# First layer of a two-level fast matrix product: six of nine steps taken in pairs with 256 moving columns, and their x^T blocks built in place

## The chip, the cores and the metric

One core of one Trainium2 chip runs the whole kernel. The metric is device time in microseconds (us) of one execution; lower is better. Three executions of the kernel before took 1302.05, 1302.54 and 1305.91 us; their median is 1302.54 us. One further execution was profiled.

## The reference

Threshold attention over 8 batches of 8 heads (576 positions, head size 64) gives x with 4608 rows of 512. Then a feed-forward block with a squared ReLU follows; all is fp32:

```python
h = np.maximum(x @ w_in, 0.0)        # 4608x512 @ 512x2048: the first layer
return (h * h @ w_out)               # 4608x2048 @ 2048x512: the output layer
```

## The kernel before

**Three stages.** Attention comes first (0 to 506 us) and writes x transposed, xT, to DRAM. The first layer runs from 506 to 900 us, the output layer from 900 us to the end. The change is in the first layer.

**First layer.** The 4608 rows are cut into nine steps of 512 (NSTEP, STEP). Each step is a two-level fast product of the kind that needs 7 block products where the plain rule needs 8: the outer level has seven indices m in the order OUTER = 1, 2, 6, 7, 4, 5, 3 (L130), and within each there are seven inner indices k, so a step has 49 products. Below, "index i" means the i-th of OUTER (i = 0 to 6), and "place (i, at)" the point in the program after the at-th product (0 to 6) of index i. A pass over all seven indices is one call of hidden_layer (L828).

**One product** (L838) takes a 128x512 weight block W_IN[m, k] (four stationary 128x128 pieces) and an x^T block of 128 rows by 128 tokens (the moving operand), so four matmuls of 128 columns fill one PSUM bank of 512 columns. In the trace every fp32 matmul is two records, each a weight load and a matmul.

**Taking results out.** `inner` (L717) runs the seven products of an index in the order k = 1, 6, 7, 5, 2, 4, 3. The banks are named X, Y, Z, W, out of a ring of six. ScalarE copies X to p1 (L752). VectorE adds Y to p1, giving u2, and Z to u2, giving u3, and then takes each finished block out of PSUM with an add (all at L125). Products 5, 6 and 7 accumulate onto X, Z and W, so product 5 waits until p1 is copied, product 6 until u3 is made, and product 7 until the first finished block, (1, 1), has been read from W. GpSimd adds earlier partial results (L125): none at index 0 (m = 1), six at index 5 (m = 5), three at every other. The temporaries p1, u2, u3 and the three sums come from a ring of six.

**Squaring.** The 16 finished blocks of a step (four each at m = 2, 4, 5, 3) are put on a list and squared six products later or more (squares_due, L823): Relu and Square on ScalarE (L819, L820), then a store of 256 KB to gT in DRAM from SP's queue (L821).

**x^T.** Each step's x^T takes four 256 KB parts from DRAM (load_x, L761) into seven slots of 512 columns, one for each m, and a side area for the three made inner kinds. There are two such regions (X_AT, L101), used in turn, so step n+1 is built while step n is multiplied. prepare_x (L789) makes 12 sums a step; each goes through sum_v (L777): ScalarE copies one operand to a PSUM buffer c (L786, two buffers), and one place later VectorE adds (L122). They run at places (2, 0) to (5, 5), one half of a sum at each place. The first step's sums are made on GpSimd during attention.

**Beside it.** 44 "chains" (L1113) make sums of w_out blocks through DRAM: a load, four GpSimd subtractions of 128x128 six to nine places later (L122), and a store at place ten. They start at places 0, 6, 12, 18, 24, 30 of a step (CHAINS, L1067). In the last step the blocks of w_out replace W_IN in SBUF (reload, L1056).

**What sets the order.** The schedule is written by hand: each engine runs its instructions in program order, and a semaphore wait holds everything behind it on that engine. All loads and stores named above go through SP's queue, in program order too. `tick` (L877), after every product, calls `also` (L1148: chains and x^T sums) and then squares_due.

Of the kernel before, what the change touches and what calls it, by code (L numbers as in the profile page):

```python
# [48 lines left out]
def kernel(  # L49
# [25 lines left out]
    nc = tc.nc  # L75
    B, H, S, D = q.shape
    P = 128
# [7 lines left out]
    BANK = 512  # L85
    MAIN = FULL * P
    STEP = 512
    NSTEP = B * S // STEP
# [6 lines left out]
    gT = [[dram.tile([P, BANK], FP32, name=f"g{n}_{j}") for j in range(16)] for n in range(NSTEP)]  # L95
# [25 lines left out]
    def minus(e, out, x, y):  # L121
        e.tensor_tensor(out=out, in0=x, in1=y, op=ALU.subtract)  # L122
# [10 lines left out]
    AT_A, AT_B = ((1, 2), (7, 4)), ((1, 7), (2, 3))  # L133
# [4 lines left out]
    W_IN, W_OUT = {}, {}  # L138
# [619 lines left out]

    XPARTS = ((0, 0), (1, 0), (1, 1), (0, 1))

    def load_x(n, parts=XPARTS):  # L761
        at = X_AT[n % 2]
        xo = arena[:, ds(at, 7 * BANK)].rearrange("p (m c t) -> p m c t", m=7, c=2)
        for a, c in parts:
            to = xo[:, AT_B[a][c] - 1, :, :]
# [9 lines left out]
        prepared[n] = (xo, None)  # L775

    def sum_v(op, out, x, y):  # L777

        c = b_pool.tile([P, BANK], FP32, tag="b", name="c")
        n = 1
        for m in y.shape[1:]:
            n *= m
        c = c[:, 0:n].rearrange("p (a b) -> p a b", b=y.shape[2])
        nc.scalar.copy(c, y)  # L786
        return lambda: op(nc.vector, out, x, c)

    def prepare_x(n, add):  # L789
# [19 lines left out]
                    yield  # L809
        prepared[n] = of  # L810

    hid = Region(arena, 0, 26 * BANK)
    squares, clock = deque(), {"n": 0}
    def hidden_bank():
# [2 lines left out]
    def square(n, j, o):  # L817

        nc.scalar.activation(out=o, in_=o, func=AF.Relu)  # L819
        nc.scalar.activation(out=o, in_=o, func=AF.Square)  # L820
        nc.sync.dma_start(out=gT[n][j][:, :].rearrange("p (k t) -> p k t", k=4), in_=o)  # L821

    def squares_due(wait):  # L823

        if squares and squares[0][0] + wait <= clock["n"]:
            square(*squares.popleft()[1:])

    def hidden_layer(n, also):  # L828

        of = prepared.pop(n)  # L830
        tile4 = lambda tag, bufs: hid.tile([P, 4, NQ], FP32, tag=tag, bufs=bufs)
        bank = lambda: hidden_bank()[:, :].rearrange("p (k t) -> p k t", k=4)
        temp = lambda name: tile4("t", 6)
        U2, U3 = {}, {}

        for m in OUTER:

            def product(to, k, more):  # L838
                for j in range(4):
                    nc.tensor.matmul(  # L840
                        to[:, j, :], W_IN[m, k][:, ts(j, P)], of[k][:, m - 1, :], start=(not more and j == 0), stop=True,
                        skip_group_check=True,
                    )

            def add(to, c, other, more, t=None):

                if other is None:
                    plus(nc.vector, to, c, more)
                else:
                    plus(nc.gpsimd, to, t, more)  # L850

            def final(ab, c, other):
                if m == 1:
                    U2[ab] = tile4("u", 12)
                    if other is None:
                        nc.scalar.copy(U2[ab], c)
                    else:
                        plus(nc.vector, U2[ab], c, other)
                    return
                t = None  # L860
                if other is not None:
                    t = temp("t")
                    plus(nc.vector, t, c, other)
                if m == 6:
                    add(U2[ab], c, other, U2[ab], t)
                elif m == 7:
                    U3[ab] = tile4("u", 12)
                    add(U3[ab], c, other, U2[ab], t)
                else:
                    o = tile4("o", 8)  # L870
                    add(o, c, other, U3[ab] if m in (4, 5) else U2[ab], t)
                    if m == 5:
                        add(U2[ab], c, other, U2[ab], t)
                    row, col = {2: (0, 0), 4: (1, 0), 5: (1, 1), 3: (0, 1)}[m]
                    squares.append((clock["n"], n, 4 * (2 * row + ab[0]) + 2 * col + ab[1], o))

            def tick(at):  # L877
                clock["n"] += 1
                also(m, at)
                squares_due(6)  # L880

            inner(product, copy, temp, bank, final, tick)


# [132 lines left out]
    with tc.manual_schedule():  # L1017
# [46 lines left out]
        halves_ = [(m, k, h) for m, k in blocks_out[EARLY:] for h in range(2)]  # L1064
        chains = [((0, RAW.index(k)), c) for k in RAW for c in range(4)]
        chains += [((1, made_at(m)), c) for c in range(4) for m in OUTER]
        CHAINS = [49 * n + 6 * c for n in range(NSTEP - 1) for c in range(n == 0, 6)][0 : len(chains)]  # L1067
        QUARTER = BANK // 4
        two = lambda t: t.rearrange("p (k o) -> p k o", k=2)
        raw_out = {}  # L1070
# [58 lines left out]
                if s_ == 10:  # L1129
                    nc.sync.dma_start(out=on(4), in_=t)  # L1130

        for n in range(NSTEP):
            last = n == NSTEP - 1
            if not last:
                load_x(n + 1)
                xsums = prepare_x(n + 1, sum_v)
            else:
                load_g(0, [(m, k) for m in (7, 4, 1, 2) for k in K_ORDER])
                rest = lambda: None
                first, second_one = outer_sums(0, 5, (1, 2))  # L1140
                work = {
                    2: outer_sums(0, 5, (7,)) + outer_sums(0, 6, (7,)),
                    3: outer_sums(0, 3, (7,)) + outer_sums(0, 7, (7,)),
                    4: inner_sums(0, 1),
                    6: [rest, rest, first, rest, second_one, rest, rest],
                }

            def also(m, at):  # L1148
                i = OUTER.index(m)
                convert_out(n, 7 * i + at)  # L1150
                chain_out(n, 7 * i + at)
                if not last:
                    if 2 <= i <= 5 and at < 6:
                        next(xsums)
# [5 lines left out]
            hidden_layer(n, also)  # L1160
            if not last:
                next(xsums, None)
        for n in range(NSTEP):
            more = n + 1 < NSTEP

            def work_of(i):

                work = [] if i == 6 else inner_sums(n, OUTER[i + 1])
                if (n, i) == (0, 0):
                    work += outer_sums(0, 6, (1, 2)) + outer_sums(0, 5, (4,)) + outer_sums(0, 6, (4,))  # L1170
                if (n, i) == (0, 1):
                    work += outer_sums(0, 7, (1, 2, 4)) + outer_sums(0, 3, (1, 2, 4))
                if more and i == 4:
                    work += outer_sums(n + 1, 5) + outer_sums(n + 1, 7, (7, 1))
                if more and i == 5:
                    work += outer_sums(n + 1, 6) + outer_sums(n + 1, 7, (2, 4))
                if more and i == 6:
                    work += outer_sums(n + 1, 3) + inner_sums(n + 1, 1)
                return work

            def also(m, at):
                i = OUTER.index(m)
                if n == 0 and 7 * i + at < 10:
                    reload(39 + 7 * i + at)
                if more and (i, at) == (2 if n == 0 else 0, 0):
                    load_g(n + 1, [(m_, k) for m_ in KINDS[0:2] for k in K_ORDER])
                if at == 0:
                    work[0] = work_of(i)
                spread(work[0], at)
                if at > 4:  # L1190
                    squares_due(0)
# [47 lines left out]
```

## Time and profile before

| | |
|---|---|
| median of three runs | 1302.54 us |
| profiled execution | 1302.09 us, of which the span from the first to the last instruction is 1300.3 us |
| first layer (L840), 1764 matmuls, 3528 records | 506.0 to 900.0 us, 394.0 us |
| one step, one index, one product | 43.78 us, 6.25 us, 0.894 us |
| granted TensorE clock | 0.998 over the span |

A line of a page names the line of the kernel, the engine (PE is TensorE's matmul, PEld its weight load, DVE VectorE, ACT ScalarE, POOL GpSimd, SP the queue of transfers), the output and inputs, and the count; then busy time, the mean duration of one, and the idle time ahead of it with what ended that. A PE duration is not a cost: matmuls overlap, so the distance from one start to the next is the measure.

### The profile page before, as it was taken

To read this page: it belongs to the slowest core of one execution; us is meant where nothing else is said; L and a number is where in the kernel's file an instruction comes from. 1 tells how busy PE (TensorE), PEld (TensorE's weight loads), DVE (VectorE), ACT (ScalarE), POOL (GpSimd) and SP (SyncE) were. 2 spreads that over 40 slices of the span, in tenths; PEclk is the share of its full clock that TensorE was granted. 3 is DMA by queue.
4 is the path that set the end of the run, shared out by engine and by line. 5 is a ranking of instruction groups with operands and counts; after the bars stand their busy time and mean duration, and the time that the engine had idled before them with its cause. 6 is when DMAs were issued, how large, how long until landed. Compare 5 with 4: busy or idle time off the path is not lost.

```text
span 1300.3 us, 47830 instructions
## 1 busy us (share of the span) xinstructions
PE 1280.6 (98%) x19463; PEld 1157.1 (89%) x19463; DVE 1009.3 (78%) x2431; ACT 846.5 (65%) x1498; POOL 916.7 (71%) x1023
## 2 busy tenths in 40 slices
PE   8999999999999999999999999999999999999998
PEld 5777777777777778999999999999999999999998
DVE  6999999999999995877787778777646654665463
ACT  6999999989998984757675766575523432343240
POOL 2787787755555321977897879768777767777775
PEclk9999999999999999999999999999999999999999
DMA  6656666544333312556655765579645224522411
GB/s 154 168 144 156 161 186 183 142 106 110 82 87 78 89 33 67 164 182 222 200 166 186 227 195 164 163 280 390 218 158 163 85 84 159 162 77 91 159 34 34
DMA packets 247035, 192.12 MB, mean 148 GB/s; under 512 B 97184, under 2 KB 195488, under 8 KB 246816
## 3 DMA queue, kind: packets, MB, share of 16 engines
q1 hardware_dynamic: 245504, 188.66, 48.5%
q8 instruction: 153, 2.51, 0.8%
q14 instruction: 66, 0.54, 0.1%
q10 hardware_dynamic: 1312, 0.41, 0.1%
HBM read 116.65 MB, written 72.35 MB: 145 GB/s over the span
## 4 chain that ended last, share of the span: by engine, by line
PE 91%; ACT 4%; DVE 3%; DMA 2%; issue 1%; POOL 0%; ACTq 0%; POOLq 0%; SPq 0%; DVEq 0%
PE ph L840 30%; PE po L975 29%; PE sc L532 11%; PE sc L434 10%; PE pt L380 6%; DVE arena L452 2%; PE sc L515 2%; PE sc L398 2%; ACT arena L523 1%; ACT arena L462 1%; DMA wall<-w 1%; PE sc L380 1%; DMA g<-arena 0%; ACT arena L403 0%; PE idle L1027 0%
## 5 line engine op out<-in xcount | busy, mean ns | idle before, releaser
L125 POOL TENSOR_TENSOR arena<-arena 128x512 f32<-128x512 f32 (+1 forms) x314 | 377.7, 1222 | 133.3 <-DVE arena L125 115.2
L975 PE MATMUL po<-wall,arena 128*128 128x128 f32 x3528 | 394.9, 275 | 1.4 <-ACT arena L752 1.4
L975 PEld LDWEIGHTS po<-wall,arena 128*128 128x128 f32 x3528 | 394.3, 192 | 2.0 <-ACT arena L752 1.8
L840 PE MATMUL ph<-arena,wall 128*128 128x128 f32 x3528 | 394.2, 275 | 0.7 <-DVE arena L659 0.7
L840 PEld LDWEIGHTS ph<-arena,wall 128*128 128x128 f32 x3528 | 394.0, 192 | 0.8 <-issue 0.8
L125 DVE TENSOR_TENSOR arena<-ph,arena 128x512 f32<-128x512 f32 x378 | 256.4, 689 | 86.2 <-PE ph L840 66.3
L122 POOL TENSOR_TENSOR arena<-arena 128x128 f32<-128x128 f32 (+2 forms) x314 | 254.7, 812 | 50.2 <-DMA arena<-w 33.8
L125 DVE TENSOR_TENSOR arena<-po,arena 128x128 f32<-128x128 f32 x378 | 108.3, 290 | 167.9 <-PE po L975 163.7
L467 DVE SCALAR_TENSOR_TENSOR arena<-arena 128x576 f32<-128x576 f32 x288 | 235.4, 853 | 0.7 <-ACT arena L462 0.7
L462 ACT ACTIVATE arena<-arena 128x576 f32<-128x576 f32 x288 | 208.6, 773 | 7.5 <-DVE arena L452 4.2
L452 DVE TENSOR_SCALAR_CACHE_REDUCE arena<-sc 128x576 f32<-128x576 f32 x288 | 205.2, 748 | 10.4 <-ACT arena L523 4.2
L786 ACT COPY c<-arena 128x512 f32<-128x512 f32 (+1 forms) x303 | 173.5, 579 | 50.1 <-DVE arena L122 41.3
L532 PEld LDWEIGHTS sc<-arena 64*64 64x64 f32 x5760 | 158.8, 133 | 35.6 <-DVE arena L452 19.4
L532 PE MATMUL sc<-arena 64*64 64x128 f32 (+1 forms) x5760 | 179.3, 262 | 2.7 <-DVE arena L452 1.5
L434 PE MATMUL sc<-arena 64*64 64x64 f32 (+1 forms) x2304 | 176.5, 414 | 3.4 <-ACT arena L403 2.3
L122 DVE TENSOR_TENSOR arena<-arena,c 128x512 f32<-128x512 f32 (+1 forms) x267 | 174.9, 663 | 5.9 <-ACT c L786 4.0
L523 ACT COPY arena<-pt 128x1024 f32<-128x1024 f32 x144 | 146.4, 1017 | 27.5 <-PE pt L380 26.3
L752 ACT COPY arena<-po 128x128 f32<-128x128 f32 x63 | 16.7, 264 | 186.5 <-PE po L975 183.7
L380 PEld LDWEIGHTS pt<-ident,arena 64*128 64x128 f32 x2304 | 83.4, 139 | 40.4 <-ACT arena L523 29.3
L752 ACT COPY arena<-ph 128x512 f32<-128x512 f32 x63 | 36.6, 582 | 124.3 <-PE ph L840 123.8
L434 PEld LDWEIGHTS sc<-arena 64*64 64x64 f32 x2304 | 74.2, 134 | 41.4 <-issue 14.4
L380 PE MATMUL pt<-ident,arena 64*128 64x64 f32 x2304 | 102.3, 229 | 3.6 <-ACT arena L523 2.2
(51 smaller groups left out, 918.7 us busy)
## 6 DMA issues: line engine op xcount, KB each, us to landing
g<-arena SPq DMA_DIRECT2D x144, 256.0 KB, 2.4
arena<-g SPq DMA_DIRECT2D x144, 256.0 KB, 4.6
w<-arena SPq DMA_DIRECT2D x60, 256.0 KB, 2.4
wall<-w SPq DMA_DIRECT2D x49, 256.0 KB, 5.2
arena<-w SPq DMA_DIRECT2D x44, 256.0 KB, 3.4
arena<-in_v_dram SPq DMA_DIRECT2D x32, 288.0 KB, 4.0
out_dram<-arena SPq DMA_DIRECT2D x70, 128.0 KB, 2.3
arena<-in_q_dram SPq DMA_DIRECT2D x64, 128.0 KB, 3.9
```

What stands on the lines that cost most here:

```text
L122: e.tensor_tensor(out=out, in0=x, in1=y, op=ALU.subtract)
L125: e.tensor_tensor(out=out, in0=x, in1=y, op=ALU.add)
L380: made = nc.tensor.transpose(pt[:, r, ts(slot, HALF)], of[rows, :], ident[rows, rows])
L434: made = nc.tensor.matmul(sc[at, ds(to, count)], lhs, kT[rows, ds(at_k, count)], start=True, stop=True)
L452: made = nc.vector.tensor_scalar(out=s[:, j, :], in0=sc[:, ds(at, S)], scalar1=1.0, scalar2=None, op0=ALU.mult, op1=ALU.min, accum_out=nmx ...
L462: nc.scalar.activation(out=w[:, :, j, :], in_=of(j), func=AF.Exp, bias=nmx[:, j : j + 1], scale=-1.0)
L467: nc.vector.scalar_tensor_tensor(out=w[:, :, j, :], in0=of(j), scalar=thr[:, j : j + 1], in1=w[:, :, j, :], op0=ALU.is_le, op1=ALU.mult, a ...
L523: touch("weights", nc.scalar.copy(joined(to), whole(pt, 0, count)), at, 2 * BANK, m)
L532: made = nc.tensor.matmul(sc[ds(u * D, D), ds(5 * j * BANK + row, count)], loaded_v[i][rows, (c - (u != j)) % CH, :], wT[m][rows, ds(weigh ...
L786: nc.scalar.copy(c, y)
L840: nc.tensor.matmul(to[:, j, :], W_IN[m, k][:, ts(j, P)], of[k][:, m - 1, :], start=(not more and j == 0), stop=True, skip_group_check=True,)
L975: nc.tensor.matmul(to, g[:, j, :], w[:, j, :], start=(not more and j == 0), stop=(j == 3), skip_group_check=True)
```

## The change

The nine steps become nine passes: step 0 alone; steps 1 and 2, 3 and 4, 5 and 6 in pairs, two passes to a pair; steps 7 and 8 alone. In a pair's pass a product loads only two of the four weight pieces (half h of the output columns) and moves 256 columns, 128 of each step, in two runs that lie one region (X_SIZE) apart. So a pass still has 49 products, each filling one bank, but with two matmuls in place of four.

Since a pair holds both regions, the next pair's x^T cannot be built in a free one. It is built in place: before_x runs in the pass ahead of a pair (passes 0, 2, 4, 6) and within_x in the pair's first pass (1, 3, 5, and 7 for steps 7 and 8). Each loads a part when its slot's index m has been multiplied, and sums over both steps at once. Sums still go through sum_v, one half of one at each place (advance_x). The sums for m = 1 and 2 run at places (5, 6) to (6, 6) of the pass ahead; those for m = 6 and 7 at (0, 6) to (1, 6), for m = 4 and 5 at (2, 4) to (3, 4), and for m = 3 at (4, 0) to (5, 0). One outer difference a step goes to GpSimd, at place (0, 1).

The squarings of m = 3, the last index, are due four products later (LATER). A pair's block holds two steps, so its store is two of 128 KB, in runs of 128 columns. Chains start at places 6, 12, 18, 24, 36 and 45 of a pass (the last as -4 of the next). The attention stage and the output layer's instructions stay.

```diff
+    def part_x(steps, k, m, count=None):
+        of = slice((steps[0] + 1) % 2, (steps[0] + 1) % 2 + len(steps))
+        ms = slice(m - 1, m - 1 + count) if count else m - 1
+        if k in (1, 7, 2, 3):
+            return places_x[:, of, ms, k in (2, 3), k in (7, 3), :]
+        return sums_x[:, of, (5, 6, 4).index(k), ms, :]
...
+    def outer_x(steps, op, o, x, y):
+        return [lambda n=n: sum_v(op, slot_x(n, o), slot_x(n, x), slot_x(n, y)) for n in steps]
+
+    def inner_x(steps, m, count=2):
+        of = lambda k: part_x(steps, k, m, count)
+        return [
+            lambda op=op, o=o, x=x, y=y: sum_v(op, of(o), of(x), of(y))
+            for op, o, x, y in ((minus, 5, 7, 1), (minus, 7, 3, 7), (plus, 6, 7, 1), (minus, 4, 2, 6))
+        ]
...
+    BEFORE_X = {(1, 0): (1, 1), (2, 0): (3, 2), (2, 1): (7, None), (3, 6): (2, 2), (6, 0): (3, 5)}
+
+    def before_x(steps, i, at):
+        if (i, at) in BEFORE_X:
+            ask_x(steps, *BEFORE_X[i, at])
...
+        if i == 4 and at < len(steps):
+            nc.scalar.copy(slot_x(steps[at], 7), slot_x(steps[at], 6))
+        work = {
+            (3, 0): lambda: turned_()[0:1], (3, 3): lambda: turned_()[1:],
+            (4, 2): lambda: added()[0:1], (4, 5): lambda: added()[1:],
+            (5, 1): lambda: fourth()[0:1], (5, 4): lambda: fourth()[1:],
+            (5, 6): lambda: inner_x(steps, 1),
+        }
+        return work.get((i, at), list)()
+
+    def within_x(steps, i, at):
+        if (i, at) == (0, 0):
+            ask_x(steps, 3, 3)
+        if (i, at) == (0,1):
+            for n in steps:
+                minus(nc.gpsimd, slot_x(n, 5), slot_x(n, 5), slot_x(n, 6))
+        work = {
+            (0,6): lambda: inner_x(steps, 6),
+            (2,4): lambda: inner_x(steps, 4),
+            (4, 0): lambda: inner_x(steps, 3, 1),
+        }
+        return work.get((i, at), list)()
+
+    LATER = {3: 4}
...
+    def advance_x():
+        if half_made:
+            half_made.pop()()
+        elif waiting:
+            half_made.append(waiting.popleft()())
...
+        for s_, step in enumerate(steps):
+            nc.sync.dma_start(
+                out=gT[step][j][:, ds(h * BANK // 2, BANK // 2)].rearrange("p (k t) -> p k t", k=2),
+                in_=o.rearrange("p (k s) t -> p k s t", s=2)[:, :, s_, :],
+            )
...
             def product(to, k, more):
+                if h is not None:
+                    for j in range(2):
+                        nc.tensor.matmul(
+                            to[:, 2 * j : 2 * j + 2, :], W_IN[m, k][:, ts(2 * h + j, P)], part_x(steps, k, m),
+                            start=(not more and j == 0), stop=True, skip_group_check=True,
+                        )
+                    return
...
-                    squares.append((clock["n"], n, 4 * (2 * row + ab[0]) + 2 * col + ab[1], o))
+                    squares.append((clock["n"] + LATER.get(m, 0), n, 4 * (2 * row + ab[0]) + 2 * col + ab[1], o))
...
-        CHAINS = [49 * n + 6 * c for n in range(NSTEP - 1) for c in range(n == 0, 6)][0 : len(chains)]
+        CHAINS = [49 * n + c for n in range(NSTEP - 1) for c in (-4, 6, 12, 18, 24, 36)[n == 0:]][0 : len(chains)]
...
+        PASSES = [((0,), None)] + [((n, n + 1), h) for n in (1, 3, 5) for h in range(2)]
+        PASSES += [((n,), None) for n in (7, 8)]
+        for n, (steps, h) in enumerate(PASSES):
             last = n == NSTEP - 1
...
+            group = (n, n + 1) if n == 7 else steps
+            ahead = (n + 1, n + 2) if n in (0, 2, 4, 6) else ()
...
+                if ahead:
+                    waiting.extend(before_x(ahead, i, at))
+                if 0 < n < 8 and h != 1:
+                    waiting.extend(within_x(group, i, at))
+                advance_x()
```

More of the change, by code (lines that the diff above doesn't have):

```diff
@@ L759, with load_x @@
     XPARTS = ((0, 0), (1, 0), (1, 1), (0, 1))
-    def load_x(n, parts=XPARTS):
+    def load_x(n, parts=XPARTS, slot=None):
         at = X_AT[n % 2]
@@ new lines, in ask_x @@
+    def ask_x(steps, m, slot):
+        (part,) = [(a, c) for a, c in XPARTS if AT_B[a][c] == m]
+        for n in steps:
+            load_x(n, [part], slot_x(n, slot))
+    BEFORE_X = {(1, 0): (1, 1), (2, 0): (3, 2), (2, 1): (7, None), (3, 6): (2, 2), (6, 0): (3, 5)}
+    def before_x(steps, i, at):
+        if (i, at) in BEFORE_X:
+            ask_x(steps, *BEFORE_X[i, at])
+        turned_ = lambda: outer_x(steps, minus, 6, 2, None)
+        added = lambda: outer_x(steps, plus, 6, 6, 1)
+        fourth = lambda: outer_x(steps, minus, 4, 2, 6)
+        if i == 4 and at < len(steps):
[7 more added lines that the diff above has]
+        return work.get((i, at), list)()
@@ new lines, in within_x @@
+    def within_x(steps, i, at):
+        if (i, at) == (0, 0):
+            ask_x(steps, 3, 3)
+        if (i, at) == (0,1):
+            for n in steps:
+                minus(nc.gpsimd, slot_x(n, 5), slot_x(n, 5), slot_x(n, 6))
[6 more added lines that the diff above has]
+    LATER = {3: 4}
+    waiting, half_made = deque(), []
@@ L838, in product @@
             def product(to, k, more):
+                if h is not None:
[4 more added lines that the diff above has]
+                        )
+                    return
+                x = of[k][:, m - 1, :] if of else part_x(steps, k, m)[:, 0, :]
                 for j in range(4):
                     nc.tensor.matmul(
-                        to[:, j, :], W_IN[m, k][:, ts(j, P)], of[k][:, m - 1, :], start=(not more and j == 0), stop=True,
+                        to[:, j, :], W_IN[m, k][:, ts(j, P)], x, start=(not more and j == 0), stop=True,
                         skip_group_check=True,
@@ L1130, in chain_out @@
                     nc.sync.dma_start(out=on(4), in_=t)
-        for n in range(NSTEP):
+        PASSES = [((0,), None)] + [((n, n + 1), h) for n in (1, 3, 5) for h in range(2)]
+        PASSES += [((n,), None) for n in (7, 8)]
+        for n, (steps, h) in enumerate(PASSES):
             last = n == NSTEP - 1
[L1134 to L1137, printed above, removed]
+            group = (n, n + 1) if n == 7 else steps
+            ahead = (n + 1, n + 2) if n in (0, 2, 4, 6) else ()
+            if last:
                 load_g(0, [(m, k) for m in (7, 4, 1, 2) for k in K_ORDER])
@@ L1158, in also @@
                     reload(7 * i + at - 10)
-            hidden_layer(n, also)
-            if not last:
-                next(xsums, None)
+            hidden_layer((steps, h), also)
         for n in range(NSTEP):
```

30 lines of the change are left out of this document (22 added, 8 removed).

## The prediction

> **What bounds the kernel now.** I read four views: the page's busy shares and chain of waits, then the waits inside the first layer, then busy time by stretch, then the groups by form.
>
> ```profile
> PE 1280.6 (98%) x19463; PEld 1157.1 (89%) x19463; DVE 1009.3 (78%) x2431; ACT 846.5 (65%) x1498; POOL 916.7 (71%) x1023
> ...
> PE 91%; ACT 4%; DVE 3%; DMA 2%; issue 1%; POOL 0%; ACTq 0%; POOLq 0%; SPq 0%; DVEq 0%
> PE ph L840 30%; PE po L975 29%; PE sc L532 11%; PE sc L434 10%; PE pt L380 6%; DVE arena L452 2%; PE sc L515 2%; PE sc L398 2%; ACT arena L523 1%; ACT arena L462 1%; DMA wall<-w 1%; PE sc L380 1%; DMA g<-arena 0%; ACT arena L403 0%; PE idle L1027 0%
> ```
>
> All 394 us of the first layer (30% of 1300) lie on the path as PE time. The waits from 506 to 900 us say whether anyone holds PE up there:
>
> ```profile
> ACT arena L752 <- PE ph L840: 123.8, 39, 5.7
> DVE arena L125 <- PE ph L840: 66.3, 133, 2.3
> ...
> POOL arena L122 <- DMA arena<-w: 33.8, 7, 5.6
> ...
> DVE arena L125 <- ACT arena L752: 5.3, 16, 0.4
> DVE arena L125 <- POOL arena L125: 4.5, 7, 0.7
> ...
> PE ph L840 <- DVE arena L659: 0.7, 1, 0.7
> ```
>
> PE waits once, 0.7 us at the start, and never again. The others wait for PE. So a shorter PE stream shortens the layer one for one, until a helper runs out of slack. The busy time of two stretches of 43.8 us (one step) shows how much they have:
>
> ```profile
> 593.60:637.40 43.80, 43.80 (x395) 43.80 (x393) 34.21 (x55) 29.02 (x53) 36.56 (x46) 1.00 0.62 193
> 637.40:681.20 43.80, 43.80 (x395) 43.80 (x394) 34.21 (x55) 28.94 (x53) 36.57 (x46) 1.00 0.62 193
> ```
>
> The columns are PE, PEld, DVE, ACT and POOL, then the granted clock (full) and the DMA share. POOL at 83% is the fullest helper, DVE has 78%.
>
> **PE's part: the gain.** The rows that price a matmul, by form:
>
> ```profile
> L840 PE MATMUL ph<-arena,wall 128*128 128x128 f32 x3528 | 394.2, 275 | 0.7 <-DVE arena L659 0.7
> L840 PEld LDWEIGHTS ph<-arena,wall 128*128 128x128 f32 x3528 | 394.0, 192 | 0.8 <-issue 0.8
> ...
> L125 DVE TENSOR_TENSOR arena<-ph,arena 128x512 f32<-128x512 f32 x378 | 256.4, 689 | 86.2 <-PE ph L840 66.3 <-ACT arena L752 5.3 <-POOL arena L125 4.5
> ...
> L532 PE MATMUL sc<-arena 64*64 64x128 f32 x4608 | 175.7, 273 | 1.4 <-DVE arena L452 0.2
> L434 PE MATMUL sc<-arena 64*64 64x512 f32 x1152 | 160.0, 609 | 3.1 <-ACT arena L403 2.3 <-ACT arena L657 0.5
> ```
>
> 394.0 / 3528 = 111.69 ns from one record's start to the next, with no gap anywhere. Is that paid by column or by record? The trace has no 256-column matmul and no full-array one but 128 wide, so I take the start times of other widths. Attention's matmuls run four at a time in 64x64 corners; in dense stretches a group starts 58 ns after the last at 64 columns (L434), 109 at 128 (L532) and 431 or 432 at 512 (L434, after dense work). From 128 to 512: (431.6 - 111.7) / 384 = 0.833 ns a column; the rest, 111.69 - 128 x 0.833 = 5.0 ns, is paid once a record. The 64-column weights at 128 columns (109 ns) also show that it is the columns that fill the time, not the loads: half the weight columns saved almost nothing.
>
> So 256 columns take 111.69 + 128 x 0.833 = 218.3 ns. The built program has 392 + 784 matmuls of 128 columns in the single passes, as before, and 588 of 256 in place of 1176 of 128: 1176 records of 218.3 ns for 2352 of 111.69. Sum: 262.70 - 256.75 = **5.9 us less**. A product takes 0.873 us in a pair's pass (0.894 before), an index 6.11, a pass 42.8.
>
> Bounds: nothing, if the extra follows the columns after all (2 x 111.69); 11.8 us, if the whole fixed part of both halves went (213.3 ns). On the other side, 512-column groups that begin after a pause stand 480 ns apart, 48 more; a pair's matmuls paying that would cost 1176 x 43 = 51 us. It occurs only where the weight load came after a gap, and here each is issued a record ahead, so I leave it out of the sum. No PE row reads a moving operand in two runs. The nearest is DVE's x^T sums (L122): 679 ns for 512 numbers, be they contiguous or in runs of 128 a region apart by slots; I take no cost.
>
> The row for 128 columns is also what the Trainium skill gives (TensorE: Matmul & The Clock Gate, Back-to-back issue gap): N / 2.4 + 2.5 ns for a pass, twice for fp32. The same section has a sustained figure, about 81 ns at N = 128 and 131 at N = 512. By it a pass at 256 would take an estimated 98, and the pairs 1176 x 2 x (2 x 81 - 98) = 151 us less. The trace disagrees: 111.7 and 432 ns a record are 56 and 216 a pass.
>
> **The helpers' part: what has to stay hidden.** Evictions keep number and form (42 DVE adds and 21 POOL adds a pass). x^T: two steps took 24 copies on ACT and 24 sums on DVE; a pair takes 24 copies, 22 sums and 2 POOL subtractions (2 x 1.27 us in 85 us). Squares: 32 instructions a pass as before. So totals fit: POOL 36.6 + 1.3 = 37.9 of 42.8 us. What counts is where they bunch.
>
> *The boundary ahead of a pair* (passes 0, 2, 4, 6). At indices 5 and 6 ACT has two p1 copies, six copies for sums (three at index 6, where there were none) and eight squares. Start to start, the trace has 0.47 us for p1, 0.49 for a c copy, 0.65 + 0.54 = 1.19 for a square: 0.94 + 2.94 + 9.52 = 13.4 us. From the first p1 at 0.95 (times from index 5's start) that ends at 14.35. The next pass starts at 12.22 and its first product ends at 13.1, so p1 is 1.25 us late and done at 14.95. u2 and u3 (0.60 apart, 0.69 long) end at 16.3; product 6, which needs u3, starts at 16.6. It fits by 0.3 us. The four squarings of m = 3 (4.8 us) would follow that p1 at once; put off, they leave ACT time to catch up. Two lines of before, at the start of a step (637.36), show POOL's tail and the 0.34 us that ACT had to spare:
>
> ```profile
> 636.78 4.97 POOL L125 TENSOR_TENSOR arena<-arena 128x512 f32<-128x512 f32 x4
> ...
> 638.49 0.59 ACT L752 COPY arena<-ph 128x512 f32<-128x512 f32 x1 [0.34 <-PE ph L840]
> ```
>
> *DVE at index 6:* six adds and four sums, 10 x 0.60 = 6.0 of 6.11 us; before, index 5 had ten in 6.25. The read of W must end before product 7 starts, 5.24 us into the index; by the same spacings it ends at 4.7. *DVE at index 1 of the pair* is alike; the sum for k = 6 of m = 6 is done some 0.2 us before its product. *POOL:* the first row above ends 4.4 us into the step; two subtractions more end at 4.7 + 2.5 = 7.2. The sum that overwrites what they read stands at place (1, 2), about 9.4.
>
> *SP and DMA.* Loads of x^T grow from 8 to 12 parts a pair, stores from 32 of 256 KB to 64 of 128 KB: some 40 issues of 0.32 to 0.46 us more in 85 us. A 2 KB packet takes 88 ns, a 512 B one 29, so a block's store takes 14.8 in place of 11.3 us of engine time; the share rises from 0.62 to about 0.72. Loads of x^T land in 2.4 to 5.5 us and are asked 6 places (5.2 us) or more ahead; the tightest, for place (3, 0), is asked at (2, 1), and if it came 1 us late at each boundary it would cost up to 4 us. The chains that move change no engine's total.
>
> **The sum:** 1302.09 - 5.9 = 1296.2 by the profiled execution. The median lies 0.45 us higher, so 1296.2 to 1296.6; I say 1296.4.
>
> **Rivals.**
> *ACT late at the boundary.* With the rows' full durations (1.25 a square, 0.59 a copy) ACT's list is 14.7 us, p1 done 4.0 us into the pass, u3 at 5.35 against 4.37: 1.0 us at each of four boundaries, 1300.4. For: the margin is 0.3 us. Against: before's spacings hold to 0.05 us.
> *Slower: a chain's load holds POOL.* POOL waited 4.1 to 5.6 us for a chain's load once in each of seven steps (33.8 us above). If the load for places (6, 0) to (6, 3) comes that late, the two subtractions end at 12.8, the sum at (1, 2) and W's read behind it at 14.2, and product 7 (11.35) waits 2.8 us; at four boundaries 11.4 us, so 1307.8. It decides from 4.3 us of wait (4 x 1.5 = the gain). Against: the late loads stood behind four loads of x^T in SP's queue at a step's start; this one stands ahead of them.
> *The columns are not cheaper.* The extra follows the columns, or two runs cost what one record saves: 1302.4. Should runs cost 48 ns a record: some 1353.
> *Cheaper still:* the fixed part goes from both halves, 1290.3 (the bound of 11.8 us); the 432 ns at 512 columns, with its 5 ns, speaks against it. The skill's sustained figures would give an estimated 1151; 111.7 and 432 ns speak against that as well.
>
> **How the numbers follow.** Forecast 0.66 (1295.5 to 1298); ACT late 0.15; POOL held 0.07; no cheaper columns 0.08, with a run penalty 0.02; cheaper ones 0.02. A measurement of this kernel can tell about 0.3% (3.9 us) from no change. Faster by more: 0.66 + 0.02 + a third of ACT's case = 0.73. Within: 0.08 and the rest of ACT's = 0.18. Slower: 0.09. The range, 1294.8 to 1302.0, holds the first two cases; POOL held, no cheaper columns, the run penalty and the cheaper ones (0.19) lie outside.
>
> **What would show it.** Right: 218 ns between starts of 256-column records, a first layer of 388 us, still no wait of PE but the first. Wrong by the columns: 223 ns or more. Wrong by ACT: PE waiting for ACT L752 or DVE at the start of passes 1, 3, 5, 7. Wrong by POOL: DVE L122 waiting for POOL there. A change outside 506 to 900 us would be none of these.

## The result and the profile after

The changed kernel takes 1299.03 us (median of 9 runs, 1297.73 to 1301.52) beside 1302.77 us for the kernel before (9 runs, 1301.62 to 1305.91): 3.7 us between the medians. The ratio on record is 0.9967, 95% interval 0.9959 to 0.9976, which is 4.3 us less (3.1 to 5.3). The sum had said 5.9 less and 1296.4; the time lies inside the range given, 2.6 us above the forecast.

The profiled execution took 1300.02 us (span 1298.2). Its first layer runs from 507.76 us to 897.8. From the first matmul's start to the last one's it takes 389.78 us; before, 393.92. (The two profiled executions differ by only 2.1 us as a whole, since the attention stage ended 1.8 us later in this one.) The page after; the first line is each engine's busy time, the next two the chain of waits by engine and by line:

```profile
PE 1276.4 (98%) x18287; PEld 1117.7 (86%) x18287; DVE 1007.0 (78%) x2423; ACT 845.5 (65%) x1498; POOL 926.8 (71%) x1031
...
PE 86%; ACT 5%; DVE 4%; DMA 3%; issue 2%; POOL 0%; SPq 0%; ACTq 0%; DVEq 0%; POOLq 0%
PE po L1077 28%; PE ph L935 16%; PE sc L532 11%; PE sc L434 10%; PE ph L942 10%; PE pt L380 6%; DVE arena L452 2%; PE sc L515 2%; PE sc L398 2%; ACT arena L462 1%; ACT arena L523 1%; DMA g<-arena 1%; PE sc L380 1%; DVE arena L125 1%; DMA wall<-w 1%
```

PE's share of the chain fell from 91 to 86%. The first layer was all PE; now L935 (pairs) and L942 (single passes) together have 26% in place of 30, and VectorE, ScalarE and DMA stand in the chain between them. The same is seen in the waits from 507.7 to 897.9 us, where before PE waited once:

```profile
DVE arena L125 <- ACT arena L752: 6.7, 7, 1.1
...
DVE arena L122 <- ACT c L791: 6.5, 13, 1.3
PEld ph L935 <- DVE arena L125: 5.4, 11, 1.3
...
ACT c L791 <- DMA arena<-xT: 3.1, 3, 1.7
...
PE ph L935 <- DVE arena L125: 1.4, 3, 0.9
DVE arena L125 <- DMA g<-arena: 0.9, 1, 0.9
...
PE ph L942 <- DVE arena L659: 0.7, 1, 0.7
```

Eleven times the weight load of a pair's matmul waits for VectorE. VectorE in turn waits for ScalarE: 7 times for p1 (L752) and 13 times for a copy c (L791), three of which waited for a load of x^T. Once VectorE waited 0.9 us for a store to land. The groups by form:

```profile
L935 PE MATMUL ph<-arena,wall 128*128 128x256 f32 x1176 | 256.6, 380 | 1.8 <-DVE arena L125 1.4 <-PE ph L935 0.2
...
L942 PE MATMUL ph<-arena,wall 128*128 128x128 f32 x1176 | 132.0, 275 | 0.7 <-DVE arena L659 0.7
```

By start times, a 256-column record stands 215 or 216 ns ahead of the next, 215.83 on average where nothing waits. So the matmuls alone save 1176 x (223.37 - 215.83) = 8.9 us, half as much again as the sum had. Late starts take 4.7 us of it back (0.07 of that at the layer's start, as before). 8.9 - 4.7 = 4.2, against 393.92 - 389.78 = 4.1 measured.

The late starts, read off as the distance between starts less the usual one, fall at few places. Where a late start or a wait of PE is placed, the place names the product that starts late, counted from 0: (3, 5) is the sixth product of index 3, which needs u3, and (3, 6) the seventh, which needs W to have been read. After each wait the next record starts up to 0.10 us late too; that is counted in.

| place | passes | us |
|---|---|---|
| (3, 5) | 2, 4 | 1.14 + 0.56 |
| (6, 5), (6, 6) | 2, 4, 6 | 0.51 + 0.16 + 0.16 |
| (0, 1) | 3 | 0.46 |
| (0, 5) | 1, 5, 7 | 0.17 + 0.40 + 0.25 |
| (1, 6) | 1, 3, 5 | 0.31 + 0.48 + 0.08 |

In a second profile of the changed kernel (at the end of the experiments) the same sum is 4.0: (3, 5), (0, 5) and (1, 6) are late there too, (0, 1) and (6, 5) are not. So what one profile shows at those two places, and differences of less than 1 us between single profiles, can be scatter.

Three of them in detail. First the longest, in pass 2, by the timeline (start, length, engine, what; the idle time ahead and its end in brackets):

```profile
608.95 2.04 SPq L773 DMA_DIRECT2D arena<-xT  x4
...
615.90 1.30 ACT L791 COPY c<-arena 128x512 f32<-128x512 f32 x2 [1.73 <-DMA arena<-xT]
...
616.52 0.69 DVE L122 TENSOR_TENSOR arena<-arena,c 128x512 f32<-128x512 f32 x1 [1.33 <-ACT c L791]
617.13 2.11 DVE L125 TENSOR_TENSOR arena<-ph,arena 128x512 f32<-128x512 f32 x3
617.86 4.18 PEld L935 LDWEIGHTS ph<-arena,wall 128*128 128x128 f32 x20 [1.27 <-DVE arena L125]
```

The loads of place (2, 0) and (2, 1) are issued from 608.95 on, 2.5 to 4.0 us after index 2 began, because stores and a chain's load stand ahead of them in SP's queue. Those that this copy needs take 5.9 us to land, where the median of the 256 KB loads is near 3.9. ScalarE waits for them, VectorE for ScalarE, and u3 behind that sum on VectorE is late for product 6.

Second, the start of pass 1 (its first 256-column record starts at 551.60):

```profile
553.24 0.58 ACT L791 COPY c<-arena 128x512 f32<-128x512 f32 x1
553.75 0.58 ACT L752 COPY arena<-ph 128x512 f32<-128x512 f32 x1
...
553.85 0.69 DVE L122 TENSOR_TENSOR arena<-arena,c 128x512 f32<-128x512 f32 x1 [1.00 <-ACT c L791]
554.45 2.28 DVE L125 TENSOR_TENSOR arena<-ph,arena 128x512 f32<-128x512 f32 x3
```

p1 (L752) is done at 554.33, 2.73 us into the pass. In the row behind it u2 starts at 554.45, u3 0.79 us later and not 0.60, because it reads u2; u3 ends 4.33 us into the pass. Product 6 was due at 4.32 and starts at 4.39. Passes 3, 5 and 7 are later still; pass 5 (its first record starts at 724.60):

```profile
726.98 0.58 ACT L752 COPY arena<-ph 128x512 f32<-128x512 f32 x1
...
727.68 2.28 DVE L125 TENSOR_TENSOR arena<-ph,arena 128x512 f32<-128x512 f32 x3
```

Here p1 is done at 2.96 (2.95 and 2.96 in passes 3 and 7), u3 at 4.56, and product 6 starts at 4.61.

Third, (0, 1) of pass 3 has another cause. Its moving operand is a sum that VectorE adds at 638.80, behind an addition that waited for a store:

```profile
638.19 0.69 DVE L125 TENSOR_TENSOR arena<-ph,arena 128x512 f32<-128x512 f32 x1 [0.88 <-DMA g<-arena]
638.80 0.68 DVE L125 TENSOR_TENSOR arena<-arena,c 128x512 f32<-128x512 f32 x1
```

### The profile page after: what moved, and what is told of

Same layout as the page of the kernel before. It is cut to its first block, busy times and chain, and to the rows that moved or that the text cites. A ratio compares the mean times of both kernels' runs of the same rounds, so it can differ in the third digit from the quotient of the medians.

```text
span 1298.2 us, 45819 instructions
## 1 busy us (share of the span) xinstructions
PE 1276.4 (98%) x18287; PEld 1117.7 (86%) x18287; DVE 1007.0 (78%) x2423; ACT 845.5 (65%) x1498; POOL 926.8 (71%) x1031
## 4 chain that ended last, share of the span: by engine, by line
PE 86%; ACT 5%; DVE 4%; DMA 3%; issue 2%; POOL 0%; SPq 0%; ACTq 0%; DVEq 0%; POOLq 0%
PE po L1077 28%; PE ph L935 16%; PE sc L532 11%; PE sc L434 10%; PE ph L942 10%; PE pt L380 6%; DVE arena L452 2%; PE sc L515 2%; PE sc L398 2%; ACT arena L462 1%; ACT arena L523 1%; DMA g<-arena 1%; PE sc L380 1%; DVE arena L125 1%; DMA wall<-w 1%
## 5 line engine op out<-in xcount | busy, mean ns | idle before, releaser
L122 POOL TENSOR_TENSOR arena<-arena 128x128 f32<-128x128 f32 (+1 forms) x322 | 265.4, 825 | 23.0 <-DMA arena<-w 6.6
L935 PE MATMUL ph<-arena,wall 128*128 128x256 f32 x1176 | 256.6, 380 | 1.8 <-DVE arena L125 1.4
L935 PEld LDWEIGHTS ph<-arena,wall 128*128 128x128 f32 x1176 | 222.2, 190 | 35.9 <-DVE arena L125 5.4
L791 ACT COPY c<-arena 128x512 f32<-128x512 f32 (+1 forms) x295 | 169.0, 578 | 71.8 <-DVE arena L122 35.8
L122 DVE TENSOR_TENSOR arena<-arena,c 128x512 f32<-128x512 f32 x235 | 154.4, 666 | 11.0 <-ACT c L791 7.6
L752 ACT COPY arena<-po 128x128 f32<-128x128 f32 x63 | 16.6, 264 | 186.4 <-PE po L1077 183.7
L942 PE MATMUL ph<-arena,wall 128*128 128x128 f32 x1176 | 132.0, 275 | 0.7 <-DVE arena L659 0.7
L942 PEld LDWEIGHTS ph<-arena,wall 128*128 128x128 f32 x1176 | 131.6, 192 | 1.1 <-issue 0.8
```

Source lines behind the costliest of these rows:

```text
L935: nc.tensor.matmul(to[:, 2 * j : 2 * j + 2, :], W_IN[m, k][:, ts(2 * h + j, P)], part_x(steps, k, m), start=(not more and j == 0), stop=Tr ...
L942: nc.tensor.matmul(to[:, j, :], W_IN[m, k][:, ts(j, P)], x, start=(not more and j == 0), stop=True, skip_group_check=True,)
```

## The experiments

Unless said otherwise a run is one profiled execution, judged by the length of its first layer and its PE waits; the whole time also moves with the attention stage (the layer started between 505.8 and 510.2 us in these runs), so one whole time decides little. The changed kernel has two profiles, the first and the last but one row; read the others against both.

| run | whole time, us | first layer, us | late starts, us |
|---|---|---|---|
| the changed kernel, first profile | 1300.02 | 389.78 | 4.7 |
| sums of x^T left out | 1293.93 | 385.10 | 0.07 |
| one store of 2 KB runs | 1296.53 | 387.28 | 2.2 |
| two sums later | 1296.14 | 388.48 | 3.4 |
| squarings not put off | 1299.92 | 391.58 | 6.5 |
| squarings put off by 9 | 1304.21 | 395.23 | 10.2 |
| fourth sum late | 1299.80 | 390.64 | 5.6 |
| contiguous columns in one pair | 1299.38 | 389.11 | 4.1 |
| two loads in the output layer | 1308.91 | 387.41 | 2.4 |
| two stores of 1 KB runs | 1301.78 | 389.44 | 4.4 |
| sums without ScalarE's copies | 1305.83 | 396.48 | 11.4 |
| the changed kernel again | 1300.14, median of 8 | 388.99 | 4.0 |
| one store, step major | 1297.32, median of 6 | 389.92 | 4.9 |

**The sums of x^T left out.**

```diff
-        if i == 4 and at < len(steps):
-            nc.scalar.copy(slot_x(steps[at], 7), slot_x(steps[at], 6))
...
-            for n in steps:
-                minus(nc.gpsimd, slot_x(n, 5), slot_x(n, 5), slot_x(n, 6))
+            pass
...
-                advance_x()
+                waiting.clear()
```

> All sums of x^T for steps 1 to 8 are left out (their ScalarE copies, VectorE adds and the two GpSimd subtractions), so the first layer multiplies unsummed data; loads, stores, squarings and matmuls stay. 13 extra loads in pass 0 fill the region. Theory A (a 256-column record costs 215.8 ns everywhere, and the 4.7 us of PE waits in the changed kernel come from the bunching of the sums and from a load that they wait for): no PE wait over 0.1 us after the start, first layer 1176 x 111.7 + 1176 x 215.8 = 385.2 us. Rival B (the doubled stores hold up SP and the ring of finished blocks): waits around place (6, 5) stay, 386 us or more. Rival C (the wide matmuls stop by themselves now and then): 389 to 390 us as in the changed kernel.

Measured 385.10 us, and no late start but the layer's first. The rows by form of this run have no wait at all in the idle column of the wide matmul:

```profile
L932 PE MATMUL ph<-arena,wall 128*128 128x256 f32 x1176 | 254.0, 379 | 0.0
...
L939 PE MATMUL ph<-arena,wall 128*128 128x128 f32 x1176 | 131.7, 275 | 0.7 <-DVE arena L659 0.7
```

So the gain of the wide matmuls is 8.8 us of a layer of 393.9, and none of the 4.7 us of late starts comes about without the sums of x^T. That the wide matmuls stop by themselves is refuted; that the stores alone hold PE up is too.

**One store of 2 KB runs for a pair's block.**

```diff
-        for s_, step in enumerate(steps):
-            nc.sync.dma_start(
...
+        nc.sync.dma_start(out=gT[steps[h]][j][:, :].rearrange("p (k t) -> p k t", k=4), in_=o)
```

> A pair's block is stored by one transfer of 256 KB in 2 KB runs, as before the change, so it lands in the wrong places of gT and the output layer reads wrong numbers. Theory A: the stores are not the cause; PE waits stay near 4.7 us, first layer 389 to 390.5 us. Rival B (64 stores of 128 KB in 512-byte runs in place of 32 keep SP and the DMA engines busy, so x^T loads come late): the waits at place (3, 5) of passes 2 and 4 (1.7 us) go and those at the boundaries shrink, 387.5 us or less.

387.28 us: rival B, in this profile. The waits at (3, 5) are gone, 1.7 us in both profiles of the changed kernel. The long ones at (6, 5) and (0, 1) are gone too, but the second profile of the changed kernel has none there either, so that says nothing of the stores. The waits of this run, to be read beside those above:

```profile
PEld ph L931 <- DVE arena L125: 3.1, 9, 0.5
...
ACT c L791 <- DMA arena<-xT: 0.2, 1, 0.2
```

In pass 2 the four loads are issued 0.3 to 2.7 us after index 2 began, in place of 2.5 to 4.0. My theory that the stores have no part in it is not borne out: 1.7 us went with the second store. How sure that is, the last experiment asks again. The 2.2 us that are left stay where they were, at (0, 5), (1, 6) and (6, 6).

**The two sums that need that load, later.**

```diff
-            (3, 0): lambda: turned_()[0:1], (3, 3): lambda: turned_()[1:],
+            (3, 2): lambda: turned_()[0:1], (3, 4): lambda: turned_()[1:],
```

> The two sums that need the part loaded at place (2, 1) stand at places (3, 2) and (3, 4) in place of (3, 0) and (3, 3). Theory A: the waits at (3, 5) of passes 2 and 4 (1.03 + 0.46 us and twice 0.10 after them) go, the others stay: first layer 388.1 us. Rival B, if the load is held by the stores ahead of it for long: the wait moves on to (3, 6) or (4, 1) and the layer stays over 389 us.

388.48 us. No wait is left at (3, 5), as expected, but pass 2 then waits 1.1 us at places (6, 4) to (6, 6), in place of the 0.5 there (0.2 in the second profile). That may be part of the lateness moved on, as rival B had it, though less than that rival's 389; one profile doesn't show it.

**Squarings of m = 3 not put off.**

```diff
-    LATER = {3: 4}
+    LATER = {3: 0}
```

> LATER is 0: the squarings of m = 3 are due as early as the others, in index 0 of the next pass. The prediction's view (put off, they leave ScalarE time to catch up at the boundary): waits at index 0 grow, by 1 to 4 us in sum, first layer 391 to 394 us. Rival D (putting them off only moves the bunch to index 1, where p1 is then late): the waits at (1, 6) of passes 1, 3 and 5 (1.1 us with what follows them) shrink and those at index 0 grow by about the same, the layer within 0.5 us of 389.8.

391.58 us, 1.8 us more than the changed kernel's first profile and 2.6 more than its second. Putting them off helps, as the prediction had it, yet not at index 0, where the expectation put the waits: the waits at (0, 5) are the same 0.17 to 0.40 us, while those at (1, 4) to (1, 6) grow to 3.2 us. The four squarings now start 3.8 us into the pass in place of 5.0 to 5.5 (pass 3), and the p1 of index 1 is done 2.7 to 3.7 us into its index in place of 2.0 to 2.4.

**Put off by 9.**

```diff
-    LATER = {3: 4}
+    LATER = {3: 9}
```

> LATER is 9 in place of 4: the squarings of m = 3 begin at place (1, 3) of the next pass. Theory A2 (ScalarE's bunching at the boundary makes about 2.2 us of the waits, the stores' 512-byte runs about 2.5): the waits at (1, 6) of passes 1, 3 and 5 go (0.3 + 0.5 + 0.1 us with the 0.10 that follows each), those at (0, 5) and (6, 6) stay; first layer 388.9 to 389.5 us. Rival D (the squarings only move the bunch): waits come up at index 2 of those passes, 389.8 us or more.

395.23 us, 5.4 more than the first profile. The waits at (1, 6) do go, but every pass that builds inner sums now waits at (2, 5), (3, 5) and (3, 6), 0.9 to 1.4 us each, and pass 6 waits 1.4 us more ahead of its end. Rival D: the bunch moves on, and p1 of index 2 is done 3.3 to 3.4 us into its index in place of 1.65 to 1.68, where m = 2's squarings stand too.

**The fourth sum behind u2 and u3.**

```diff
-            (5, 6): lambda: inner_x(steps, 1),
+            (5, 6): lambda: inner_x(steps, 1)[0:3],
...
+            (0, 1): lambda: inner_x(steps, 1)[3:],
```

> The fourth sum for m = 1 and 2 (k = 4) stands at place (0, 1) of the next pass in place of (6, 5) of the pass ahead, so that VectorE adds u2 and u3 of index 0 before it. Theory A2: the waits at (0, 5) of passes 1, 3, 5 and 7 go (0.2 + 0.4 + 0.4 + 0.25 us), the others stay; first layer 388.4 to 389 us. Rival E (it is the late p1 copy itself, not the sum ahead of u2): the waits at (0, 5) stay, 389.6 us or more.

390.64 us. The waits at (0, 5) stay, 0.15 + 0.23 + 0.38 + 0.24 us: rival E, the late p1 itself. Most of the rest is the wait for the load, here 1.64, 0.56 and 1.03 us at (3, 5) of passes 2, 4 and 6; it differs from execution to execution.

**One run of 256 columns in one pair.**

```diff
-                            to[:, 2 * j : 2 * j + 2, :], W_IN[m, k][:, ts(2 * h + j, P)], part_x(steps, k, m),
+                            to[:, 2 * j : 2 * j + 2, :], W_IN[m, k][:, ts(2 * h + j, P)],
+                            places_x[:, 0, m - 1, k in (2, 3), :, :] if steps[0] == 3 else part_x(steps, k, m),
```

> In the pair of steps 3 and 4 the 256 moving columns are one contiguous run (of wrong numbers) in place of two runs of 128; the other pairs stay. If the width sets the cost: 215.8 ns a record in all pairs. If the two runs set it (the 5.0 ns that a record pays at 128 columns and in the 512-column rows would be paid, and the 2.5 is due to two runs): 218.3 ns in this pair alone, 1.0 us more for its two passes.

215.83 ns a record, contiguous (392 records) or in two runs (784). The width sets the cost, and two runs cost nothing.

**Gathering in the output layer.** A pair's block is stored as it lies, and two loads make a step's block of it.

```diff
+        nc.sync.dma_start(out=gT[steps[h]][j][:, :].rearrange("p (k t) -> p k t", k=4), in_=o)
...
+            for h in range(2):
+                of = gT[first + h][j][:, :].rearrange("p (k s t) -> p k s t", k=2, s=2)
+                nc.sync.dma_start(out=to[:, 2 * h : 2 * h + 2, :], in_=of[:, :, s_, :])
```

> A pair's block is stored by one transfer of 256 KB in 2 KB runs, as it lies, and the output layer gathers a step's block by two loads of 128 KB in 512-byte runs; results as in the changed kernel. Theory A2: the waits at (3, 5) of passes 2 and 4 and the long one at (6, 5) go, first layer 387.3 us as with the one store that put blocks in wrong places; the output layer keeps its 396 to 397 us. Rival F (the gathered loads then come late for the output layer): its waits grow by 1 us or more.

The first layer is 387.41 us as expected, but the output layer's matmuls take 405.7 us in place of 396.6: rival F. PE stands still for 4.3 and 3.5 us near 938 us, where step 1's blocks must have come, while SP issues 19 loads in one row:

```profile
924.65 13.52 SPq L1024 DMA_DIRECT2D arena<-g  x19
...
937.82 1.16 PE L1081 MATMUL po<-wall,arena 128*128 128x128 f32 x8 [4.26 <-DVE arena L126]
942.50 2.71 PE L1081 MATMUL po<-wall,arena 128*128 128x128 f32 x11 [3.52 <-ACT arena L753]
```

**Two stores of 1 KB runs.**

```diff
-                in_=o.rearrange("p (k s) t -> p k s t", s=2)[:, :, s_, :],
+                in_=o[:, 2 * s_ : 2 * s_ + 2, :],
```

> A pair's block is still stored by two transfers of 128 KB, but each takes one contiguous 1 KB run of a row in place of two runs of 512 bytes, so numbers land in wrong places of gT. If the doubled number of transfers (SP's time to issue them) makes the x^T loads late: the waits at (3, 5) of passes 2 and 4 and the long one at (6, 5) stay, first layer 389.3 to 391 us. If the short runs (the DMA engines' time) do: they go, first layer 387.3 us.

389.44 us, with 0.94 and 1.12 us at (3, 5) of passes 2 and 4. Runs of 1 KB in place of 512 bytes do not help; what helped in the two runs with one store was either the single transfer or its 2 KB runs.

**The sums at the boundary without ScalarE's copies.**

```diff
+        if m == 1:
+            return [
+                lambda op=op, o=o, x=x, y=y: lambda: op(nc.vector, of(o), of(x), of(y))
...
```

> The four sums for m = 1 and 2 at the end of a pass are added by VectorE straight from SBUF, without ScalarE's copies (4 x 0.49 us less on ScalarE ahead of each boundary). Theory E (ScalarE is late at the boundary, by its copies and squarings, and with it p1): the waits at (0, 5) of passes 1, 3, 5 and 7 go (1.2 us in sum with what follows them), those at (3, 5) stay, first layer 388.0 to 389.2 us; a sum takes about 0.68 us as with the copy. Rival G (VectorE and GpSimd slow each other when both read two operands from SBUF): a sum takes 1 us or more, and waits at (6, 5) and (6, 6) grow, 390 us or more.

396.48 us: rival G. Busy times by form from 510 to 900 us, sums with the copy first, then those straight from SBUF, subtractions and additions:

```profile
L122 DVE TENSOR_TENSOR arena<-arena,c 128x512 f32<-128x512 f32 x44 | 29.9, 679 | 5.0 <-ACT c L791 3.1 <-DMA w<-arena 1.6
L122 DVE TENSOR_TENSOR arena<-arena 128x512 f32<-128x512 f32 x12 | 15.2, 1266 | 0.0
...
L125 DVE TENSOR_TENSOR arena<-arena 128x512 f32<-128x512 f32 x4 | 6.3, 1583 | 0.0
```

A sum of two SBUF operands takes 1.27 us (subtractions) and 1.58 (additions) on average in place of 0.68. The late starts at places (6, 5) and (6, 6) grow to 4.8 us.

The trace also bears out rival G's reason. The 16 sums take anything from 0.81 to 1.79 us, and each ends 0.55 us after the end of the GpSimd instruction under way when it began. The other way round, the eleven GpSimd sums of 512 columns that begin during such a sum take 1.71 to 1.74 us; the others take 1.26 to 1.31. One of each, by the timeline from 729.5 to 732.5 us:

```profile
729.15 0.99 POOL L122 TENSOR_TENSOR arena<-arena 128x128 f32<-128x128 f32 x2
...
729.88 0.81 DVE L122 TENSOR_TENSOR arena<-arena 128x512 f32<-128x512 f32 x1
730.09 1.73 POOL L125 TENSOR_TENSOR arena<-arena 128x512 f32<-128x512 f32 x1
```

By this trace the two engines take turns at such work, and the price depends on what GpSimd is doing. The copy that loads ScalarE is worth its price.

**One store, step major, and the changed kernel beside it.** The matmul writes its two runs of 128 columns so that a step's half is 1 KB in a row, and both steps' blocks are in one DRAM tensor.

```diff
-                            to[:, 2 * j : 2 * j + 2, :], W_IN[m, k][:, ts(2 * h + j, P)], part_x(steps, k, m),
+                            to.rearrange("p (s k) t -> p s k t", s=2)[:, :, j, :], W_IN[m, k][:, ts(2 * h + j, P)], part_x(steps, k, m),
...
+            out=gP[steps[0]][j][:, ds(h * BANK // 2, BANK // 2)].rearrange("(s p) c -> p s c", s=2),
+            in_=o.rearrange("p (s k) t -> p s (k t)", s=2),
```

> A pair's matmul writes its 256 columns as two runs of 128 (step major) into the PSUM bank, so a step's half of a block is one run of 1 KB; both steps' blocks lie in one DRAM tensor, and one transfer of 256 KB stores both halves. The output layer's loads stay as they were. Theory H (the doubled number of stores in SP's queue makes x^T loads late; ScalarE's bunch makes the rest): the waits at (3, 5) of passes 2 and 4 and the long one at (6, 5) go, those at (0, 5), (1, 6) and (6, 6) stay (2.2 us in sum), first layer 387.3 us, 2.5 us less than the changed kernel, and 6.5 to 7 us under the kernel before. Rival I (writing in two runs costs the matmul something): a record takes more than 215.8 ns and the layer is over 388 us.

> The changed kernel once more, as the yardstick for the kernel beside it on the same chip. Nothing is changed: first layer 389 to 391 us, with PE waits of 4 to 5.5 us; 3.5 to 5 us faster than before.

On one chip, five rounds: before 1303.97 us (14 runs); the changed kernel 1300.14, ratio 0.9971 (0.9960 to 0.9981); the single store 1297.32, ratio 0.9950 (0.9939 to 0.9962). The medians are 2.8 us apart and the intervals barely overlap: by this run the single store is faster than both kernels. A record stays at 215.8 ns, so rival I's cost of writing in two runs is refuted. Theory H is not borne out: its layer of 387.3 us was measured at 389.9. The profile does not show why the kernel is faster: the profiled execution was the slowest of its six (1299.71 us), and in it the loads of pass 2 took 6.7 to 7.0 us to land (where the trace has the landing) though they were issued sooner (1.8 to 3.4 us after index 2 began), and PE waited 1.47 us at (3, 5). The waits of the two profiles, the changed kernel first:

```profile
PEld ph L935 <- DVE arena L125: 5.1, 11, 1.3
ACT c L791 <- DMA arena<-xT: 3.1, 3, 1.8
```

```profile
PEld ph L942 <- DVE arena L133: 5.5, 11, 1.6
ACT c L799 <- DMA arena<-xT: 3.8, 4, 2.1
```

They are alike. That the single store's other executions had no such wait fits their times (1296.1 to 1298.5) but was not seen. Over all profiles in which the sums that need that load stand where the changed kernel has them, (3, 5) is late by 1.4 to 3.2 us in sum in each one with two stores, by about 0.1 at most in two with a single store, and by 1.9 in this third one. Open, then: whether the number of transfers, their run length or chance decides how long a load takes to land; issue times did fall in all three profiles with a single store.

## Why the prediction held, and where its steps failed

**PE bounds the layer, and a shorter stream shortens it.** Right: with the sums out, 8.8 us of matmul time came off the end.

**256 columns take 218.3 ns.** The direction held, the size was off: 215.83, so 8.9 us in place of 5.9. The step that was mis-sized is the fixed part of a record: at the prediction's 0.833 ns a column, 215.83 = 256 x 0.833 + 2.5, so it is 2.5 ns and not 5.0. (The two full-array widths alone fit 0.814 ns a column and 7.5 fixed as well; the runs don't separate the two.) The row that had it stood in the prediction: 128 columns with 64-column weights, 109 ns, are 2.4 over the columns' time. I took the full-array row because its shape was nearest, and did not ask why two rows of one width differ. The Trainium skill's form (TensorE: Matmul & The Clock Gate, Back-to-back issue gap) charges 2.5 ns a pass, hence an estimated 5.0 for a record, taken as two passes; at 128 columns this trace agrees with 111.7 ns, at 256 it shows 2.5 a record, and the measurement decides. Two runs cost nothing, as assumed.

**The helpers fit.** This failed, by 4.7 us in this profile and 4.0 in the other. The two errors partly cancelled: 3.0 us too little gain, 4.7 too few waits. That the time lies inside the range is luck in part: without the waits it would have been an estimated 1294.4 (1299.03 - 4.7), below the range, and the run without the sums took 1293.93. It lies above the 1295.5 to 1298 of the forecast itself. And one of the prediction's own signs of being wrong came up: PE waits for VectorE early in passes 1, 3, 5 and 7.

*The boundary.* "p1 done at 14.95", that is 2.73 us into the pass, holds in pass 1 alone, behind the slower pass 0; at passes 3, 5 and 7 it was 2.95 to 2.96, 0.22 later. The margin of 0.3 us behind it was not there even in pass 1. The sum spaced u2 and u3 by 0.60 us, as VectorE's other adds are; u3 reads u2 and starts 0.79 after it. So u3 ended at 4.33 in place of 4.08 (4.56 in the later passes), and product 6 was due 0.05 sooner, at 4.32, since a product takes 0.863 us. PE waited 0.17 to 0.40 us there in passes 1, 5 and 7. The rival "ACT late at the boundary" named the chain that stopped PE, but with 1.0 us at each of four boundaries, from a p1 done at 4.0; p1 came at 2.73 to 2.96, and the waits at (0, 5) sum to 0.8 us in this profile and 1.2 in the other.

*"DVE at index 6."* W's read was to end 4.7 us into the index. By the same spacing of 0.79 and the sum ahead of it, it ended at 5.18 (passes 4 and 6), when product 7 was due: 0.16 us late in each.

*"DVE at index 1 of the pair is alike."* It is not: the squarings put off land there, p1 of index 1 is late (VectorE waited 0.86 us for it in pass 1), and W is read late for product 7. The two runs that moved the squarings show it from both sides. The change's own remedy, four products, is the best of the three tried (0, 4, 9).

*Place (3, 0).* Named as the tightest load, with up to 4 us if it came late; I left it at nothing because loads had landed in 2.4 to 5.5 us. What I did not add was SP's queue ahead of it: two steps' stores, a chain's load and two earlier loads put the issue 2.5 to 4.0 us behind the start of index 2, and the landing took up to 6.1 us. It cost 1.7 us, of the up to 4 that the prediction named.

**Rivals.** A chain's load holding POOL did not occur: POOL's waits for chains fell from 33.8 to 6.6 us. The columns did get cheaper, against the third rival. Outside the layer no change stands out: the output layer's matmuls take 396.1 us before and 396.6 after (396.5 in the second profile).

## What to carry to other kernels

Widening the moving operand pays a few nanoseconds for each record saved (here 7.5), and the price is best taken from all widths in the trace, with their fixed parts side by side. Where an engine that was fully hidden has 0.3 us to spare by a sum of durations, count it as late: an add that reads the one before it, and a faster stream, use that up, and each wait costs up to a tenth of a microsecond more. When a load's deadline is checked, add what stands ahead of it in its queue to its landing time, and expect the landing itself to vary by a microsecond or more. A copy that keeps VectorE from reading two SBUF operands beside a busy GpSimd can be worth its time.

## What the runs showed of the hardware

An fp32 record of 256 columns costs 2.5 ns over its columns' time at 0.833 ns each, one of 128 with full weights 5.0; why is not explained. After most waits the second record starts about 104 ns late again (320 ns in place of 216; in the single passes 214 in place of 112), some 1.1 us of the 4.7. On VectorE, 128x512 adds of 0.69 us start 0.60 us apart, but at least 0.79 where one reads the other's result (u3 after u2). With both operands in SBUF, a 128x512 sum on VectorE beside a busy GpSimd takes 0.81 to 1.79 us and ends 0.55 us after the GpSimd instruction that was under way; a 512-column GpSimd sum begun meanwhile takes 1.7 us in place of 1.3. With one operand in PSUM the VectorE sum takes 0.68. The loads of x^T at places (2, 0) and (2, 1) of pass 2 landed in 4.7 to 5.3 us in one profile and in 6.7 to 7.0 in another.
